# Making the convolution taps in 64 by 128 blocks instead of 32 by 64, with the tables laid out anew

## The chip, the cores and the metric

The kernel runs on one core of one Trainium2 chip, in one launch. The metric is the device time of an execution in microseconds (us), lower is better; three executions of the kernel before gave 542.96, 544.31 and 545.70 us, so the median is 544.31. A profile of one further execution shows what each engine did: PE is the matrix engine (PEld its weight loads), DVE the vector engine, ACT the scalar engine, POOL the general engine, SP the one that issues most DMAs.

## What is computed

The input is a sequence of 2048 positions and 448 channels. Two mixers work on it and a gate adds them:

```
q = (x @ wq).reshape(16 heads, 28);  k = x @ wk;  v = x @ wv      # one k and v for all heads
a = softmax(q k^T / sqrt(28)) v, heads side by side, @ wo
dt = exp(log_dt);  A = A_re + i A_im                              # 448 channels x 256 states
K[d, l] = Re sum_n C[d,n] * dt*B[d,n] * exp(dt*A[d,n] * l)        # 2048 taps for each channel
y[l, d] = sum_{m<=l} K[d, m] u[l-m, d]  +  Dskip[d] u[l, d]       # causal convolution
g = sigmoid(sum(x * gate_w));   out = g * a + (1 - g) * y
```

So there is an attention with 1024 score tiles (4 query blocks x 16 heads x 16 key tiles, each 128 keys by 512 queries), and a state space model whose 448 x 2048 taps are made first and then applied as a long convolution.

## The kernel before, in words

**Attention.** A loop over sets of three and two score tiles: PE multiplies keys by queries into PSUM (L1103 or L1112), ACT takes the exponential of the set in one instruction (L1134), PE multiplies by the values (L1144) into one bank. After 16 key tiles of four heads DVE copies the sums out (L1004), the denominators are inverted by way of POOL's DMAs (denT, R, rdenB), and DVE scales (L1014). `qproj` makes the queries of the next block, `outp` and `tail` multiply by `wo` (L986, L1055), and `fold` adds the gated result to O (L995).

**Convolution.** The 448 channels are worked in 14 chunks of 32. For each chunk:

- `masters` (L780, for a block of chunks) squares the complex numbers z = exp(dt A) again and again (L796 to L816), so that z to the powers 1, 2, 4 ... is at hand in bf16.
- `tables` (L820) builds on DVE, for 128 states in the partitions, two halves of states and 32 channels in the free dimension, the powers needed. Both the plain powers and those times C dt B stand in a table of rows, one row of EW = 128 elements for each of 32 exponents: 64 plain (half, channel) and 64 weighted. Real and imaginary part are two blocks, BLK = 33 rows apart. Five levels double the table: at each, L850 multiplies by the real part of a power, L852 by the imaginary part, and L854 and L856 subtract and add. The sizes go from 256 to 4096 elements (multiplications) and 128 to 2048 (additions). L859 and L863 build the decays `rho`, L867 multiplies them with the table in one instruction of 4096 elements (the mirrored powers, `Fm`), L872 changes a sign. Two tables alternate; `Fm` is there once.
- `kgen` (L875) makes the taps. The 2048 taps of a channel are the 32 by 64 outer product over 256 states, real and imaginary: four matmuls of 32 stationary columns (weighted powers) and 64 moving columns (plain and mirrored powers). Neighbouring columns are one row apart, 256 bytes. Four channels lie side by side in the four column groups of the array. A chunk takes 128 matmuls and fills one PSUM bank. DVE adds Dskip to one tap of each channel (L899) and copies the rest (L902) to `kstg`, and POOL issues nine DMAs that write them to DRAM (`KP_scratch`).
- `conv` (L937, twice a chunk) lets SP load the taps back as Toeplitz tiles, 1 MB for four channels (`tload`, into four buffers in T and, late in the run, three in U), and PE multiplies them with the input (L949) into a bank `ps`. DVE scales by 1 - g (L958) to `cst`, PE transposes by small matmuls (L969) into another bank `px`, DVE adds to O (L977).

**Order.** Nothing is ordered by hand. Each instruction is put on a list with its dependencies, an estimated duration and a priority `pr` (small is urgent: 0 for the scores, 1.4 taps, 1.6 convolution, 2 evictions, 50 and more for the tables), and `schedule` (L156) simulates the engines with these estimates and fixes the order of each engine before the program is emitted. `lock` and `unlock` hand out the two PSUM banks of POOL = (7, 5) (psX and the last of psS) that `qproj`, `kgen`, `conv`, `outp` and `prep` share; every other bank belongs to the attention. FETCH is its estimate for the loading of a block of 256 PE instructions while DMAs are running; SLACK is added to the time from which an instruction of priority 2 or more on an engine is taken to be ready. Real durations do not change the order: an engine stands where its next instruction must wait. At the end `tail` (L1040) writes O out.

Of the kernel before, what the change touches and what calls it, by code (L numbers as in the profile page):

```python
# [24 lines left out]
BLK = 33 * EW  # L25
LO = 2 * BLK
# [48 lines left out]
class Prog:  # L75
# [6 lines left out]
    BLOCK, FIRST, FETCH, IDLE, NEED = 256, 172, 5300.0, 3300.0, 0.015  # L82
# [3 lines left out]
    SLACK = {"pe": 500.0, "dve": 300.0}  # L86
# [289 lines left out]
class Kernel:  # L376
# [25 lines left out]
    def alloc(self):  # L402
        nc = self.nc
        sb = self.sb
        self.psS = self.ps("psS", 3072)
        self.psB = self.ps("psB", 512)
        self.psX = self.ps("psX", 512)
        self.psSb, self.psBb, self.psXb = self.psS.cast(BF), self.psB.cast(BF), self.psX.cast(BF)
        self.xT = sb("xT", XQ, BF)
        self.qM = sb("qM", 2 * 4 * 512, BF)  # L410
        self.kT = sb("kT", S, BF)
        self.vaug = sb("vaug", 512, BF)
        self.Wq = sb("Wq", NT * 512, BF)
        self.Wo = sb("Wo", NT * D, BF)
        self.Wb = sb("Wb", P, BF)
        self.ident = sb("ident", P, BF)
        self.qT = sb("qT", 2 * 512, BF)
        self.expT = sb("expT", RING * 512, BF)
        self.Wk = Sub(self.expT, (RING - 1) * 512)
        self.Wv = Sub(self.expT, (RING - 2) * 512)  # L420
        self.Wm = Sub(self.expT, (RING - 2) * 512 + 128)
        self.acc = sb("acc", 2 * 512, F32)
        self.rdenB = sb("rdenB", 512, F32)
        self.denT = sb("denT", 16, F32)
        self.onT = sb("onT", 4 * 512, BF)
        self.omq = sb("omq", 128, F32)
        self.U = sb("U", D * 32, BF)
        self.O = sb("O", 16 * D, BF)
        self.T = sb("T", NTR * TW + 768, BF)
        self.tab = sb("tab", 2 * LO + 32 * EW, BF)  # L430
        self.tmp = sb("tmp", 2 * 8 * EW, BF)
        self.rho = self.tmp
        self.mbf = sb("mbf", BM * MC, BF)
        self.mq = sb("mq", 5 * W2, BF)
        self.msq = sb("msq", 2 * 64 * BM, F32)
        self.msr = self.tmp.cast(F32)
        self.identf = self.msq
        self.seedz = sb("seedz", 2 * W2, F32)
        self.seedw = sb("seedw", 2 * W2, BF)
        self.kstg = sb("kstg", 2 * 256, BF)  # L440
        self.cst = sb("cst", 2 * 512, BF)
        self.skt = sb("skt", D // 4, BF)
        self.small = sb("small", 16, F32)
        self.gt = sb("gt", 2 * 16, F32)
        self.KP = nc.dram_tensor("KP_scratch", (2 * KH,), BF).ap()
        self.XS = nc.dram_tensor("XS_scratch", (3 * DT * XQ,), BF).ap()
        self.R = nc.dram_tensor("R_scratch", (16 * 4 * 512,), F32).ap()
# [37 lines left out]
    def loads(self):  # L485
# [57 lines left out]
        for k in range(2, 6):  # L543
# [4 lines left out]
        pg.dma([(self.skt.v(32 * g + 31, 1, 0, [[8, 14], [1, 8]]), dram(ins["B_Dskip"], 8 * g, [[16 * D, 1], [32, 14], [1, 8]]))  # L548
                for g in range(4)], (112, 8), "sk", rd=["skt"], wr=["skt"], pr=1, slow=True)
# [121 lines left out]
    def prep_params(self):  # L671
# [71 lines left out]
        for s in range(2):  # L743
            o = s * LO + 32 * EW
            for comp, val in ((0, 1.0), (1, 0.0)):
                pg.op("dve", lambda e, o=o, comp=comp, val=val: e.memset(self.tab.v(0, P, o + comp * BLK, [[1, 64]]), val), 70,
                      wr=[("lo", s, 0)] + xd, pr=3)
# [32 lines left out]
    def masters(self, b):  # L780
# [13 lines left out]
        for k in range(11):  # L794
# [20 lines left out]
            off = k * 256 if k < 5 else (k - 6) * 256 + 64  # L815
# [4 lines left out]
    def tables(self, c):  # L820
# [6 lines left out]
        mq = lambda lv: self.mq.v(0, P, lv * W2 + 64 * c, [[1, 64]])  # L827
        pr = 50 + 2 * c

        def vo(fn, n, rd, wr, rate=1.92):  # L830
# [3 lines left out]
        vo(lambda e: e.tensor_copy(tab.v(0, P, lo + 31 * EW, [[BLK, 2], [1, 64]]), mbf.v(0, P, mo, [[128, 2], [1, 64]])),  # L834
           128, [("mb", 0), lk(0)], [lk(1)])
        vo(lambda e: e.tensor_copy(tab.v(0, P, lo + 31 * EW + 64, [[BLK, 2], [1, 64]]),
                                   self.seedw.v(0, P, c * 64, [[W2, 2], [1, 64]])),
           128, [("w32", b), ("w32b", b), lk(0)], [lk(2)])
        done = [lk(1), lk(2)]
        for lv in range(5):  # L840
# [3 lines left out]
            so, do = lo + (32 - w) * EW, lo + (32 - 2 * w) * EW  # L844
            src = tab.v(0, P, so, [[BLK, 2], [EW, w], [1, EW]])
            dst = tab.v(0, P, do, [[BLK, 2], [EW, w], [1, EW]])
            mr = mbf.v(0, P, m, [[0, 2], [0, w], [1, EW]])
            mi = mbf.v(0, P, m + 128, [[0, 2], [0, w], [1, EW]])
# [3 lines left out]
            vo(lambda e, src=src, mi=mi, w=w, tb=tb, to=to: e.tensor_tensor(  # L852
                tb.v(0, P, to, [[w * EW, 2], [EW, w], [1, EW]]), src, mi, ALU.mult), 2 * n, done + mk(lv), [tk])
            vo(lambda e, do=do, n=n, tb=tb, to=to: e.tensor_tensor(  # L854
                tab.v(0, P, do, [[1, n]]), tab.v(0, P, do, [[1, n]]), tb.v(0, P, to + n, [[1, n]]), ALU.subtract), n, [tk, kr], [kr])
            vo(lambda e, do=do, n=n, tb=tb, to=to: e.tensor_tensor(  # L856
                tab.v(0, P, do + BLK, [[1, n]]), tab.v(0, P, do + BLK, [[1, n]]), tb.v(0, P, to, [[1, n]]), ALU.add), n, [tk, ki], [ki])
            done = done + [kr, ki]
        vo(lambda e: e.tensor_copy(rho.v(0, P, 31 * 64, [[1, 64]]), mq(0)), 64,  # L859
           [("mq", 0)], ["tmp"])  # L860
        for lv in range(5):
            w = 1 << lv
            vo(lambda e, w=w, lv=lv: e.tensor_tensor(rho.v(0, P, (32 - 2 * w) * 64, [[64, w], [1, 64]]),  # L863
                                                     rho.v(0, P, (32 - w) * 64, [[64, w], [1, 64]]),
                                                     self.mq.v(0, P, lv * W2 + 64 * c, [[0, w], [1, 64]]), ALU.mult), w * 64,
               [("mq", lv), "tmp"], ["tmp"])
        vo(lambda e: e.tensor_tensor(tab.v(0, P, FM, [[64, 2], [EW, 32], [1, 64]]),  # L867
                                     tab.v(0, P, lo + 31 * EW, [[BLK, 2], [-EW, 32], [1, 64]]),
                                     rho.v(0, P, 31 * 64, [[0, 2], [-64, 32], [1, 64]]), ALU.mult), 4096,
           done + ["tmp"], ["Fm"])  # L870
        ni = tab.v(0, P, lo + BLK + EW, [[EW, 31], [1, 64]])
# [3 lines left out]
    def kgen(self, c):  # L875
# [4 lines left out]
        G = self.grp()  # L880
        keys = self.tabkeys
        for jj in range(8):
            def mm(e, comp, jj=jj):
                for half in range(2):
                    for g in range(4):
                        o = half * 32 + 8 * g + jj
                        fo = lo + comp * BLK + EW + o
                        mo = FM + comp * 64 + o
                        r = e.matmul(  # L889
                            G.v(32 * g, 32, 64 * jj, [[1, 64]]),  # L890
                            tab.v(0, P, lo + comp * BLK + 64 + o, [[EW, 32]]),
                            tab.v(0, P, fo, [[mo - fo, 2], [EW, 32]]),
                            start=(comp == 0 and half == 0), stop=(comp == 1 and half == 1),
                            tile_position=(0, 32 * g), skip_group_check=True)
                return r
            for comp in range(2):
                pg.op("pe", lambda e, mm=mm, comp=comp: mm(e, comp), 226, mode="c", ni=16, rd=keys,
                      wr=[X, "kst", "kst2"], pr=1.4, lock=G if jj == 0 and comp == 0 else None)
        pg.op("dve", lambda e: e.tensor_tensor(self.kstg.v(0, P, 63, [[64, 8]]), G.v(0, P, 63, [[64, 8]]),  # L899
                                               self.skt.v(0, P, 8 * c, [[1, 8]]), ALU.add),  # L900
              el(8), rd=[X, "skt"], wr=["kst"], pr=2)
        pg.op("dve", lambda e: e.tensor_copy(self.kstg.v(0, P, 0, [[64, 8], [1, 63]]), G.v(0, P, 0, [[64, 8], [1, 63]])),  # L902
              el(504), rd=[X], wr=["kst2"], pr=2, unlock=G)
        ko = self.kstg
        rs = ko.rs
        lst = [(dram(self.KP, 32 * c * KW + 1024, [[8 * KW, 4], [KW, 8], [1, 64]]),
                bass.AP(tensor=ko.h, offset=16 * rs, ap=[[32 * rs, 4], [64, 8], [1, 64]]))]
        for g in range(4):
            for h in range(2):
                lst.append((dram(self.KP, h * KH + (32 * c + 8 * g) * KW, [[64, 16], [KW, 8], [1, 64]]),  # L910
                            ko.v(32 * g + 16 * h, 16, 0, [[64, 8], [1, 64]])))
        pg.dma(lst, (1056, 128), "kw", rd=["kst", "kst2"], wr=[("KP", c)], pr=0, eng="pool", extra=4000)
# [24 lines left out]
    def conv(self, c):  # L937
# [3 lines left out]
        ps, px = self.grp(), self.grp()  # L941
        for k in range(4):
# [3 lines left out]
            for n in range(8):  # L946
# [14 lines left out]
              el(512), rd=[X, "omq"], wr=[("cst", cs)], pr=2, unlock=ps)  # L961
# [12 lines left out]
        for k in range(4):  # L974
            pg.op("pe", lambda e, k=k: yt(e, k), 70, mode="h", ni=8, rd=[("cst", cs), "id"], wr=[Y], pr=1.55, lock=px if k == 0 else None)
# [4 lines left out]
    def outp(self, qc, tt):  # L980
# [4 lines left out]
        for g in range(4):  # L985
# [3 lines left out]
                rd=["Wo"] + [("on", gg) for gg in range(4)], wr=[X], pr=2, lock=G if g == 0 else None)  # L989
# [239 lines left out]
```

## Time and profile before

| | us |
|---|---|
| median of three executions | 544.31 |
| profiled execution | 546.33 |
| its span, first to last instruction | 544.5 |
| busy: ACT, DVE, PE | 485.9, 455.3, 451.6 |
| first exp to last exp (L1134) | 30.5 to 523.2 |
| DMA: 144.55 MB, mean rate | 265 GB/s |
| taps of the first chunk start, of the last end | 83.5, 484.8 |

A row of instruction groups reads: line, engine, operation, output <- inputs by the program's names, shapes (partitions x elements, type), count | busy us in all, mean ns of one | idle us of the engine just before them, and what ended it. For matmuls "128*32 128x64" is 128 rows by 32 stationary columns, and 128 by 64 moving. Of the chain that ended last, ACT has 30%, PE 27%, DVE 19% and DMA 15%.

### The profile page before, as it was taken

What the parts mean: (1) busy time and instruction counts of PE and PEld (TensorE: products, weight loads), DVE (VectorE), ACT (ScalarE), POOL (GpSimd) and SP (SyncE); (2) the same over time, 40 slices, a digit from 0 to 9 for tenths busy, and PEclk for the clock granted to TensorE, in tenths of its full rate; (3) what the DMA queues carried; (4) which work ended last, traced back from release to release, by engine and by line L of the source; (5) the groups of instructions that cost most, each with busy time, mean ns of one, the idle gap of its engine ahead of it and who ended that gap; (6) DMA issues with size and microseconds to landing.
All of it is one profiled execution on the core that took longest, in us unless ns stands there. A gap on an engine that the chain in (4) does not pass through costs nothing.

```text
span 544.5 us, 20905 instructions
## 1 busy us (share of the span) xinstructions
PE 451.6 (83%) x9463; PEld 226.4 (42%) x9479; DVE 455.3 (84%) x826; ACT 485.9 (89%) x431; POOL 168.1 (31%) x313
## 2 busy tenths in 40 slices
PE   4787679688798989789788898889898898996875
PEld 3522114154353535345344445345454444352443
DVE  2889999999999989889989998989899999912024
ACT  3699899999999989899999999999999998997840
POOL 5017022515142413315215241515225060532100
PEclk9958888999999999899999999999899999998888
DMA  8995691696977697896994998798994999679996
GB/s 254 238 232 151 47 159 30 172 355 206 360 238 247 189 368 244 257 365 216 361 373 136 362 308 305 208 390 273 326 371 144 345 337 353 182 258 321 361 385 194
DMA packets 122401, 144.55 MB, mean 265 GB/s; under 512 B 54196, under 2 KB 60956, under 8 KB 122312
## 3 DMA queue, kind: packets, MB, share of 16 engines
q1 hardware_dynamic: 112312, 133.06, 75.9%
q0 software_dynamic: 9344, 9.59, 7.3%
q8 instruction: 74, 1.21, 0.9%
q10 hardware_dynamic: 656, 0.57, 0.4%
q14 instruction: 15, 0.12, 0.1%
HBM read 128.76 MB, written 5.28 MB: 246 GB/s over the span
## 4 chain that ended last, share of the span: by engine, by line
ACT 30%; PE 27%; DVE 19%; DMA 15%; issue 3%; SPq 0%
ACT expT L1134 30%; DMA T<-KP_scratch 9%; PE psS L1112 6%; DMA U<-KP_scratch 6%; PE psX L889 5%; PE psS L1103 4%; PE psB L1144 4%; PE psS L949 2%; PE psX L949 2%; DVE msq L796 2%; DVE tab L850 2%; DVE mbf L816 2%; DVE seedz L800 1%; PE psS L889 1%; DVE tmp L852 1%
## 5 line engine op out<-in xcount | busy, mean ns | idle before, releaser
L1134 ACT ACTIVATE expT<-psS 128x1536 bf16<-128x1536 f32 (+1 forms) x410 | 468.1, 1317 | 23.1 <-PE psS L1112 11.7
L1112 PE MATMUL psS<-qM,kT 128*32 128x512 bf16 x1660 | 134.3, 400 | 14.0 <-ACT expT L1134 10.6
L1103 PE MATMUL psS<-qT,kT 29*128 29x512 bf16 x609 | 82.9, 400 | 33.4 <-ACT expT L1134 29.6
L1144 PE MATMUL psB<-expT,vaug 128*32 128x512 bf16 x1024 | 104.7, 398 | 0.7 <-issue 0.4
L135 POOL DMA_DIRECT2D KP_scratch<-kstg x126 | 67.8, 546 | 70.7 <-DVE kstg L902 69.2
L850 DVE TENSOR_TENSOR tab<-tab,mbf 128x256 bf16<-128x256 bf16 (+4 forms) x70 | 68.6, 979 | 0.7
L1103 PEld LDWEIGHTS psS<-qT,kT 29*128 29x128 bf16 x609 | 19.9, 91 | 83.3 <-ACT expT L1134 72.9
L135 POOL DMA_DIRECT2D rdenB<-R_scratch x60 | 30.6, 517 | 75.8 <-DMA R_scratch<-denT 56.3
L889 PE MATMUL psX<-tab 128*32 128x64 bf16 x1280 | 49.5, 286 | 0.3 <-issue 0.2
L1112 PEld LDWEIGHTS psS<-qM,kT 128*32 128x32 bf16 x1660 | 30.4, 98 | 45.6 <-ACT expT L1134 34.7
L1144 PEld LDWEIGHTS psB<-expT,vaug 128*32 128x32 bf16 x1024 | 27.4, 96 | 49.9 <-issue 38.2
L135 POOL DMA_DIRECT2D qM<-qT x64 | 32.1, 509 | 43.4 <-DVE gt L638 20.4
L889 PEld LDWEIGHTS psX<-tab 128*32 128x32 bf16 x1280 | 39.4, 135 | 11.3 <-issue 3.9
L949 PE MATMUL psX<-T,U 128*32 128x128 bf16 (+7 forms) x1568 | 34.4, 221 | 9.0 <-DMA T<-KP_scratch 5.9
L135 POOL DMA_DIRECT2D denT<-acc x15 | 11.3, 756 | 97.5 <-DVE acc L1004 97.5
L949 PE MATMUL psS<-T,U 128*32 128x128 bf16 (+7 forms) x1216 | 30.2, 222 | 9.5 <-DMA T<-KP_scratch 6.7
L852 DVE TENSOR_TENSOR tmp<-tab,mbf 128x256 bf16<-128x256 bf16 (+3 forms) x56 | 36.3, 648 | 0.0
L949 PEld LDWEIGHTS psX<-T,U 128*32 128x32 bf16 (+7 forms) x1568 | 26.5, 94 | 20.3 <-DMA T<-KP_scratch 8.1
L867 DVE TENSOR_TENSOR tab<-tab,tmp 128x4096 bf16<-128x4096 bf16 x14 | 32.1, 2290 | 0.4
L852 DVE TENSOR_TENSOR tab<-tab,mbf 128x4096 bf16<-128x4096 bf16 x14 | 31.9, 2278 | 0.0
L949 PEld LDWEIGHTS psS<-T,U 128*32 128x32 bf16 (+7 forms) x1216 | 21.7, 95 | 21.0 <-DMA T<-KP_scratch 6.9
L863 DVE TENSOR_TENSOR tmp<-tmp,mq 128x64 bf16<-128x64 bf16 (+4 forms) x70 | 25.3, 361 | 1.2
(153 smaller groups left out, 553.4 us busy)
## 6 DMA issues: line engine op xcount, KB each, us to landing
T<-KP_scratch SPq DMA_DIRECT2D x174, 512.0 KB, 9.3
U<-KP_scratch SPq DMA_DIRECT2D x50, 512.0 KB, 9.5
rdenB<-R_scratch POOLq DMA_DIRECT2D x60, 64.0 KB
U<-cst SPq DMA_DIRECT2D x1, 3584.0 KB, 19.0
qM<-qT POOLq DMA_DIRECT2D x64, 32.0 KB, 5.2
tab<-in_A_x_dram SPq DMA_DIRECT2D x4, 448.0 KB, 6.2
O<-in_A_x_dram SPq DMA_DIRECT2D x16, 112.0 KB, 2.7
O<-cst SPq DMA_DIRECT2D x1, 1792.0 KB, 27.1
```

Of the source, the lines that this page charges most:

```text
L135: return [e.dma_start(o, i, **kw) for o, i in pairs]
L796: pg.op("dve", lambda e: e.tensor_tensor(m2(msq), z2, z2, ALU.mult), el(2 * n), rd=[kr, ki] + first, wr=["msq"], pr=pr)
L850: vo(lambda e, dst=dst, src=src, mr=mr: e.tensor_tensor(dst, src, mr, ALU.mult), 2 * n, done + mk(lv), [kr, ki])
L852: vo(lambda e, src=src, mi=mi, w=w, tb=tb, to=to: e.tensor_tensor(tb.v(0, P, to, [[w * EW, 2], [EW, w], [1, EW]]), src, mi, ALU.mult), 2 * ...
L863: vo(lambda e, w=w, lv=lv: e.tensor_tensor(rho.v(0, P, (32 - 2 * w) * 64, [[64, w], [1, 64]]), rho.v(0, P, (32 - w) * 64, [[64, w], [1, 64]]),
L867: vo(lambda e: e.tensor_tensor(tab.v(0, P, FM, [[64, 2], [EW, 32], [1, 64]]), tab.v(0, P, lo + 31 * EW, [[BLK, 2], [-EW, 32], [1, 64]]), r ...
L889: r = e.matmul(G.v(32 * g, 32, 64 * jj, [[1, 64]]), tab.v(0, P, lo + comp * BLK + 64 + o, [[EW, 32]]), tab.v(0, P, fo, [[mo - fo, 2], [EW, ...
L949: r = e.matmul(ps.v(32 * j, 32 - 2 * n, 128 * k, [[1, 128]]), self.U.v(0, P, (4 * gi + j) * 32 + 2 * n, [[1, 32 - 2 * n]]), tbuf.v(0, P, t ...
L1103: r = e.matmul(self.psS.v(0, P, 512 * b, [[1, 512]]), kT.v(32 * h, DH + 1, 128 * kt, [[1, 128]]), qT.v(32 * h, DH + 1, 512 * (i % 2), [[1, ...
L1112: r = e.matmul(self.psS.v(32 * j, 32, 512 * b, [[1, 512]]), kT.v(0, P, 128 * kt + 32 * j, [[1, 32]]), self.qM.v(0, P, (i % 2) * XQ + 512 * ...
L1134: pg.op("act", lambda e: e.activation(expT.v(0, P, 512 * es[0], spread(es, n)), self.psS.v(0, P, 512 * bs[0], spread(bs, n)), AF.Exp, scal ...
L1144: r = e.matmul(self.psB.v(32 * h, 32, 0, [[1, 512]]), vaug.v(0, P, 32 * kt, [[1, 32]]), expT.v(0, P, 512 * ring[t], [[1, 512]]), start=(kt ...
```

## The change

The tables get another layout. A row now belongs to a pair of channels (and a half of the states) and holds all 32 exponents, each as two real and two imaginary parts: element 128 * row + 4 * exponent + 2 * part + channel of the pair. Rows 0 to 31 are weighted, rows 32 to 63 plain, so that the exponents of neighbouring pairs follow each other in steps of 4 elements (8 bytes) without a gap. Additions and the mirrored product now take two elements of every four; the mirrored product is split in two of 2048 elements, and a copy of 124 elements restores the entries for exponent 0 of the constant table.

A tap matmul takes 64 stationary columns (the 32 exponents of one channel in each of two pairs) and 128 moving columns (those two pairs, plain and mirrored), so its 64 by 128 result holds four blocks of 32 by 64, of which the two on the diagonal are taps of one channel. Two such matmuls lie side by side in two column groups. A chunk takes 64 matmuls and fills two banks, which are taken, evicted and given back one after the other; L899 and L902 come twice. The DMA that writes the taps becomes ten issues.

In `conv`, `px` is now the bank of `ps`. The projections in `outp` go from priority 2 to 1.2, FETCH from 5300 to 6200, SLACK of DVE from 300 to 500 ns. The core of the diff:

```diff
-    BLOCK, FIRST, FETCH, IDLE, NEED = 256, 172, 5300.0, 3300.0, 0.015
+    BLOCK, FIRST, FETCH, IDLE, NEED = 256, 172, 6200.0, 3300.0, 0.015
-    SLACK = {"pe": 500.0, "dve": 300.0}
+    SLACK = {"pe": 500.0, "dve": 500.0}
...
-            src = tab.v(0, P, so, [[BLK, 2], [EW, w], [1, EW]])
-            mr = mbf.v(0, P, m, [[0, 2], [0, w], [1, EW]])
+            src = tab.v(0, P, so, [[EW, 64], [2, 2 * w], [1, 2]])
+            dc = [tab.v(0, P, do + 2 * k, [[EW, 64], [4, w], [1, 2]]) for k in range(2)]
+            mr = mbf.v(0, P, m, [[2, 64], [0, 2 * w], [1, 2]])
...
+            tc = [tb.v(0, P, to + 2 * k, [[4 * w, 64], [4, w], [1, 2]]) for k in range(2)]
+            vo(lambda e, dc=dc, tc=tc: e.tensor_tensor(dc[0], dc[0], tc[1], ALU.subtract), n, [tk, kr], [kr])
+            vo(lambda e, dc=dc, tc=tc: e.tensor_tensor(dc[1], dc[1], tc[0], ALU.add), n, [tk, ki], [ki])
...
-        vo(lambda e: e.tensor_tensor(tab.v(0, P, FM, [[64, 2], [EW, 32], [1, 64]]),
+        for k in range(2):
+            vo(lambda e, k=k: e.tensor_tensor(tab.v(0, P, FM + 2 * k, [[EW, 32], [4, 32], [1, 2]]),
+                                              tab.v(0, P, lm + 124 + 2 * k, [[EW, 32], [-4, 32], [1, 2]]),
+                                              rho.v(0, P, 62, [[64, 32], [-2, 32], [1, 2]]), ALU.mult), 2048,
...
+        vo(lambda e: e.tensor_copy(tab.v(0, P, lm + EW, [[EW, 31], [1, 4]]), tab.v(0, P, lo + 64 * EW, [[0, 31], [1, 4]])),
+           124, done + ["Fm"], done)
...
+        for q in range(2):
+            G = self.grp()
+            for k in range(4):
+                m = 4 * q + k
...
+                                r = e.matmul(
+                                    G.v(64 * u, 64, 128 * k, [[1, 128]]),
+                                    tab.v(0, P, lo + cg * EW + 2 * comp + u, [[4, 64]]),
+                                    tab.v(0, P, fo, [[EW, 2], [mo - fo, 2], [4, 32]]),
...
+                pg.op("pe", mm, 230, mode="h", ni=16, rd=keys,
+                      wr=[(X, q), ("kst", q), ("ksk", q)], pr=1.4, lock=G if k == 0 else None)
...
-        ps, px = self.grp(), self.grp()
+        ps = px = self.grp()
...
-                rd=["Wo"] + [("on", gg) for gg in range(4)], wr=[X], pr=2, lock=G if g == 0 else None)
+                rd=["Wo"] + [("on", gg) for gg in range(4)], wr=[X], pr=1.2, lock=G if g == 0 else None)
```

## The prediction

> **What bounds the kernel now.** I read the busy times first, then the same by stage, the waits of the engines, the chain of waits, and the rows of the lines that the diff touches.
>
> ```profile
> PE 451.6 (83%) x9463; PEld 226.4 (42%) x9479; DVE 455.3 (84%) x826; ACT 485.9 (89%) x431; POOL 168.1 (31%) x313
> ```
>
> Three engines are within 6% of each other over the span. By stage (start:end, length, busy us and instructions of PE, PEld, DVE, ACT, POOL, then clock, DMA share, GB/s):
>
> ```profile
> 300.00:327.00 27.00, 25.26 (x539) 12.31 (x540) 26.24 (x45) 27.00 (x25) 9.57 (x17) 1.00 0.98 338
> 436.00:463.00 27.00, 23.60 (x569) 12.63 (x566) 24.54 (x39) 24.62 (x22) 9.47 (x19) 1.00 1.00 345
> 463.00:490.00 27.00, 25.85 (x615) 13.29 (x614) 14.97 (x23) 26.97 (x25) 11.43 (x22) 1.00 0.68 219
> 490.00:504.00 14.00, 8.83 (x160) 3.60 (x152) 3.85 (x7) 10.64 (x10) 3.98 (x8) 0.86 1.02 322
> ```
>
> Up to 477 us DVE and ACT are both nearly full and PE is close behind; after it DVE idles. There are two races. **Attention**: 410 exps run from 30.5 to 523.2 us with about 24.6 us of gaps between them; normalisation and output projection take the 21 us left. **The long convolution**: DVE makes the tables of 14 chunks one after another (the last step, L872, ends at 476.4), PE turns each into taps, POOL writes these to DRAM, SP loads them back as Toeplitz tiles, PE convolves. The last chunk's taps start at 477.2 and end at 484.8, and the chain after that is mostly loads, by the chain of waits (start, us, what):
>
> ```profile
> 491.68 11.99 DMA U<-KP_scratch
> ...
> 515.39 11.49 DMA U<-KP_scratch
> ...
> 538.74 0.61 PE psX L949 x32
> ```
>
> So what delays the tables delays the end, unless the 68 us behind them shrink. The DVE waits between 109 and 463 us (us in total, times, longest) show how little room DVE has:
>
> ```profile
> DVE cst L958 <- PE psS L949: 4.1, 3, 1.6
> DVE acc L1004 <- PE psB L1144: 3.5, 4, 1.7
> DVE O L977 <- PE psX L969: 2.3, 2, 1.6
> DVE O L995 <- PE psS L986: 1.8, 1, 1.8
> DVE cst L958 <- PE psX L949: 1.6, 4, 0.6
> DVE O L995 <- PE psX L986: 1.2, 1, 1.2
> ```
>
> With the smaller ones that is 16.3 us in 354; DVE stands only where the written order makes it await PE.
>
> **DVE, the added work.** The rows that price it (busy us, mean ns, idle before):
>
> ```profile
> L867 DVE TENSOR_TENSOR tab<-tab,tmp 128x4096 bf16<-128x4096 bf16 x14 | 32.1, 2290 | 0.4
> L854 DVE TENSOR_TENSOR tab<-tab 128x2048 bf16<-128x2048 bf16 x14 | 17.0, 1212 | 0.0
> L902 DVE CAST kstg<-psX 128x504 bf16<-128x504 f32 x10 | 6.7, 673 | 0.0
> L834 DVE COPY tab<-mbf 128x128 bf16<-128x128 bf16 x14 | 2.6, 186 | 0.0
> L899 DVE TENSOR_TENSOR kstg<-psX,skt 128x8 bf16<-128x8 f32 x10 | 1.9, 186 | 7.0 <-PE psX L889 6.9
> ```
>
> Two of the four blocks in each new product are unused, so a chunk fills two banks and is evicted twice: 673 + 186 = 859 ns more. The 4096-wide product becomes two of 2048: 2 x 1212 - 2290 = 134 ns. The new copy of 124 elements is one 186 ns copy. Together 1.18 us a chunk, x14 = 16.5 us, and 56 more instructions with the 7 ns that separate unheld ones (4.3 us in some 595 gaps) make 16.9. Nothing hides this: DVE is the engine that is full.
>
> **DVE, the same work in the new layout.** Element counts of the ten multiplications, ten additions, five decay steps and the sign change stay. Additions, the two products and the sign change now touch two adjacent bf16 and skip two (8-byte steps); multiplications read contiguous tables but a repeated pair as their factor. No row of before has such a DVE operand. Lower bound: nothing, as the type and the pairs stay. It is not less, since no operand of before has runs under 64 elements that could gain. Upper bound: one element a cycle instead of two, as in the f32 rows (682 - 414 ns for 256 elements, 1.05 ns each, against 0.52 in the bf16 rows, (1212 - 683)/1024). The skipping operations stream 2 x 3968 + 4096 elements a chunk, 6.2 us, so 6.2 us more a chunk, 87 us in all; the multiplications, 2 x 7936 elements, could add another 8.3 us a chunk. I take nothing: the nearest row is bf16 by two operands, L854. The few first levels may cost 50 ns each; they lie inside the range.
>
> [...]
>
> **PE.** Two timeline rows (start, us, line, times):
>
> ```profile
> 87.54 1.07 PE L889 MATMUL psS<-tab 128*32 128x64 bf16 x32
> ```
>
> ```profile
> 112.39 0.62 PE L949 MATMUL psS<-T,U 128*32 128x128 bf16 x32
> ```
>
> ```profile
> 131.02 0.45 PE L969 MATMUL psS<-ident,cst 128*64 128x64 bf16 x16
> ```
>
> Less the last one's 0.29, 0.22 and 0.20 us, a tap matmul costs 25 ns, a convolution one 13, a transposition one (two column groups, 64 stationary columns, as the new ones) 17. Today's taps, with elements 256 bytes apart, take 100 ns for four of 64 columns, 128 x 25 = 3.2 us a chunk. The new: 64 matmuls of 128 columns in two groups. At the convolution's rate a pair takes 52 ns, 26 each, 1.7 us; at today's strided rate 200 ns a pair, 6.4 us. I take twice the transposition's 17 ns, 34 ns: 2.2 us, a gain of 1.0 us a chunk, 14 us of PE time, because that row has the groups, the stationary width and a short step (4 bytes) in its moving operand. It is mostly off the path; where it is on it, it shortens ACT's and DVE's waits for PE. The pieces "issue" of 1.0 to 1.6 us on PE just behind the dense taps (336, 411, 455, 461 us) can shrink too: 128 of some 1,300 PE instructions a chunk go.
>
> **Other parts.** The tap write has ten issues instead of nine: 0.53 us more on POOL's queue a chunk, behind it the denT, qM and R transfers, before which POOL sits idle for longer than that (97.5 us in ten waits before denT alone); on the path only for the last chunk, 0.5 us. The convolution in one bank adds no wait: its transposition already awaits the eviction that frees the bank. But taps now need two banks in turn; where a convolution awaiting its load holds the other, the second half awaits an eviction queued behind up to 2.3 us of table work. Bounds of that: nothing, as with two free banks, and 14 x 2.3 = 32 us of later taps; I take nothing on the path, since DVE works on the next table meanwhile, and keep 2 us for the last chunk in the range. The planner's new constants move evictions 0.2 us later behind their producers: 21 DVE stalls x 0.2 = 4.2 us at least; with shorter PE bursts I take half of the 16.3 us, 8 us, bounds 0 and 16. The projection moved ahead of the convolutions frees its bank earlier and costs the same: nothing, bounds -2 and 2.
>
> **Sum**, against the profiled execution, 546.33 us (span 544.5): +16.9 (DVE) - 8 (stalls) + 0.5 (write) - 3.5 (last chunk's taps, 7.6 us long, in half the pieces between the attention matmuls, 1.0 of it PE time proper) = +5.9, 552.2 us. The median of the runs, 544.31, lies 2.0 below that execution: **550**.
>
> **Rivals.** (1) PE relief wins. Of ACT's gaps some 7 us are awaited "issue" or convolution bursts; if attention ends 7 us earlier, DVE loses no time to PE (all 16) and the 68 us after the tables shrink by 10, since the buffers that stand full from 479 to 488 us (DMA share 0.68) come free sooner: 16.9 - 16 - 10 = -9, **535**. For it: PE is 96% busy in 463:490 and the loads stall there. Against: convolutions still await the last tables. It decides once stalls and tail give back over 17 us. (2) The skipping DVE operands run at one element a cycle: 87 + 6 us less a tail of 20, about **615**; with part of it, 575 to 615. It decides from 0.4 us a chunk on. (3) The halved matmuls take no less time, as the change does not do what it says: at 50 ns each PE stays at 3.2 us, DVE's 16.9 come with no relief but the write's order: about 544.3 + 13 = **557**; at 100 ns PE gets 45 us more and the time goes to 575.
>
> **Chances.** The forecast 0.41 (543 to 555), rival 1 0.33 (531 to 542), rival 2 0.14, rival 3 0.12. A measurement here tells 0.5% from no change, that is 541.6 to 547.0. Below it lie rival 1 and little else, 0.34; within it the lower part of the forecast, 0.16; above it 0.50. The range runs from 531 to 580, which leaves out the far ends of rivals 1 and 2.
>
> **What would show it.** After: L902 and L899 twice as often at 0.67 and 0.19 us; the 2048-wide additions at 1.2 us (2.3 proves rival 2); tap matmuls about 34 ns apart (50 or more: rival 3); L872 of the last chunk near 485 us; DVE stalls near 8 us; from there to the end under 68 us. I am wrong if the tables end no later than 477 us, or if the time behind them shrinks by more than they are late.

## The result, and the profile after

The changed kernel takes **562.53 us** (median of four executions, 560.1 to 564.82) against 544.65 for the kernel before beside it: ratio 1.0331, 95% interval 1.0274 to 1.0388, so 3.3% slower. Its profiled execution took 560.1 us, with a span of 558.2, 13.7 more than before; all comparisons of profiles below are between these two spans, which lie some 4 us closer together than the medians. The mean granted clock was 0.935 (0.953 before); that does not explain 18 us, since the kernel before, run beside experiment 1, took 542.8 to 547.9 us at 0.928 to 0.952.

The busy line of the page (engine, busy us, share of the span, instructions):

```profile
PE 467.2 (84%) x8567; PEld 222.6 (40%) x8583; DVE 470.5 (84%) x882; ACT 489.4 (88%) x431; POOL 175.9 (32%) x327
```

PE has 896 instructions fewer and is busy 15.6 us **longer**; DVE has 56 instructions and 15.2 us more. The busy time by stage of the changed kernel, with the columns of the table shown for before:

```profile
300.00:327.00 27.00, 25.08 (x396) 9.61 (x397) 25.97 (x47) 26.84 (x25) 9.19 (x17) 1.00 0.74 240
436.00:463.00 27.00, 25.90 (x453) 11.91 (x454) 25.38 (x49) 25.49 (x24) 10.69 (x21) 1.00 0.86 283
463.00:490.00 27.00, 24.82 (x545) 12.79 (x533) 25.67 (x44) 25.95 (x24) 9.39 (x18) 1.00 0.88 300
490.00:504.00 14.00, 10.87 (x195) 4.06 (x195) 10.77 (x17) 12.68 (x12) 2.36 (x5) 0.83 0.93 313
```

In 300:327 and 436:463 PE is as busy as before or busier with a fifth to just over a quarter fewer instructions (396 for 539, 453 for 569). In 463:490 DVE is full (25.67 us), where before it had run out of tables (14.97): the tables now end in 490:504. L875, the sign change that ends a table (L872 before), ends for the last chunk at 502.8 us, 26.4 later than the 476.4 of before.

Which rows grew? Groups by shape (busy us, mean ns of one | idle before):

```profile
L868 DVE TENSOR_TENSOR tab<-tab,tmp 128x2048 bf16<-128x2048 bf16 x28 | 34.4, 1228 | 0.7
L898 PE MATMUL psX<-tab 128*64 128x128 bf16 x448 | 33.3, 303 | 0.2 <-DVE tab L875 0.2
L898 PE MATMUL psS<-tab 128*64 128x128 bf16 x448 | 33.5, 302 | 0.0
L856 DVE TENSOR_TENSOR tab<-tab 128x2048 bf16<-128x2048 bf16 x14 | 17.1, 1221 | 0.0
L912 DVE CAST kstg<-psX 128x504 bf16<-128x504 f32 x14 | 9.5, 676 | 0.0
L856 DVE TENSOR_TENSOR tab<-tab,tmp 128x128 bf16<-128x128 bf16 x14 | 3.9, 281 | 0.0
```

The DVE rows read as priced: the addition of 2048 in 8-byte steps takes 1221 ns (1212 before), an eviction 676. The surprise is L898: 33.5 + 33.3 = 66.8 us of PE for 896 tap matmuls, where the 1792 of before had 49.5 + 19.5 = 69.0. The mean of 303 ns is the duration of one matmul's record; as several are under way at a time, it says nothing of the pace. The pace is in a timeline row (start, us, engine, line, how many):

```profile
254.88 1.16 PE L898 MATMUL psS<-tab 128*64 128x128 bf16 x16
```

Less 0.30 for the last one, 15 follow each other in 0.86 us, 57 ns apart; over all such rows 57.7. A chunk has 64 of them: 3.7 us, against 128 x 23.4 = 3.0 us by all rows of before. Halving the matmuls made the taps 0.7 us a chunk longer.

DVE's waits between 109 and 463 us, the stretch shown for before (us in total, times, longest):

```profile
DVE kstg L908 <- PE psX L898: 8.6, 10, 1.6
DVE kstg L908 <- PE psS L898: 8.5, 9, 1.8
DVE O L986 <- PE psS L978: 2.4, 1, 2.4
```

The convolution's evictions (`cst`), which led the list before, have nearly gone from it. In their place DVE stands before L908, the first of each eviction pair, until the taps are done. From 109 us to the end of the last table its waits of over 0.15 us were 21, 17.1 us in all; now they are 34, 27.3 us. ACT waits more too, over the whole span. Before (L1112 multiplies `qM`, L1103 `qT`):

```profile
ACT expT L1134 <- PE psS L1112: 11.7, 13, 2.4
ACT expT L1134 <- PE psS L1103: 8.3, 12, 1.5
```

and after, where L1112 is the old L1103 and L1121 the old L1112:

```profile
ACT expT L1143 <- PE psS L1112: 22.2, 32, 2.5
...
ACT expT L1143 <- PE psS L1121: 6.5, 17, 1.3
```

Its gaps between exps grew from 24.6 to 32.5 us, and the last exp ends at 530.2 instead of 523.2. The chain of waits at the end (start, us, what):

```profile
512.39 17.28 ACT expT L1143 x15
...
540.21 8.15 DMA U<-KP_scratch
...
548.75 2.35 issue
551.11 1.69 PE psS L958 x53
```

ACT runs without a break from 512 to 530 us and only one load is left in this part of the chain. From the last table to the end it is now 55.4 us, 12.7 less than before. Most of that is a shorter queue of loads: the last 16 of the 224 Toeplitz loads, one chunk's, start 21.0 us after the last table instead of 29.7. So tables 26.4 us later, what follows 12.7 us shorter: 13.7 us of span.

### The profile page after: what moved, and what is told of

It reads as the page before. It is cut to its first block, busy times and chain, and to the rows that moved or that the text cites. A ratio compares the mean times of both kernels' runs of the same rounds, so it can differ in the third digit from the quotient of the medians.

```text
span 558.2 us, 19186 instructions
## 1 busy us (share of the span) xinstructions
PE 467.2 (84%) x8567; PEld 222.6 (40%) x8583; DVE 470.5 (84%) x882; ACT 489.4 (88%) x431; POOL 175.9 (32%) x327
## 4 chain that ended last, share of the span: by engine, by line
ACT 44%; PE 34%; DVE 10%; DMA 9%; issue 2%; SPq 0%; ACTq 0%
ACT expT L1143 44%; PE psS L1121 7%; DMA T<-KP_scratch 6%; PE psX L898 5%; PE psS L898 5%; PE psS L1112 4%; PE psB L1153 4%; PE psS L958 2%; DMA U<-KP_scratch 1%; DMA mbf<-in_A_wq_dram 1%; PE psX L958 1%; DVE msq L795 1%; PE psX L995 1%; DVE mbf L815 1%; PE psX L758 1%
## 5 line engine op out<-in xcount | busy, mean ns | idle before, releaser
L1121 PE MATMUL psS<-qM,kT 128*32 128x512 bf16 x1660 | 136.0, 405 | 17.6 <-ACT expT L1143 14.1
L1112 PE MATMUL psS<-qT,kT 29*128 29x512 bf16 x609 | 83.9, 405 | 41.4 <-ACT expT L1143 35.8
L134 POOL DMA_DIRECT2D KP_scratch<-kstg x140 | 76.4, 554 | 57.0 <-DVE kstg L912 39.7
L1112 PEld LDWEIGHTS psS<-qT,kT 29*128 29x128 bf16 x609 | 19.9, 91 | 96.4 <-ACT expT L1143 84.9
L1121 PEld LDWEIGHTS psS<-qM,kT 128*32 128x32 bf16 x1660 | 28.6, 97 | 59.7 <-ACT expT L1143 46.1
L958 PE MATMUL psS<-T,U 128*32 128x128 bf16 (+7 forms) x1600 | 37.5, 223 | 1.6 <-DMA T<-KP_scratch 0.9
L958 PE MATMUL psX<-T,U 128*32 128x128 bf16 (+7 forms) x1184 | 30.6, 231 | 5.9 <-DMA T<-KP_scratch 3.5
L868 DVE TENSOR_TENSOR tab<-tab,tmp 128x2048 bf16<-128x2048 bf16 x28 | 34.4, 1228 | 0.7
L958 PEld LDWEIGHTS psS<-T,U 128*32 128x32 bf16 (+7 forms) x1600 | 28.2, 95 | 14.7 <-issue 4.1
L898 PE MATMUL psX<-tab 128*64 128x128 bf16 x448 | 33.3, 303 | 0.2 <-DVE tab L875 0.2
L898 PE MATMUL psS<-tab 128*64 128x128 bf16 x448 | 33.5, 302 | 0.0
L898 PEld LDWEIGHTS psX<-tab 128*64 128x64 bf16 x448 | 24.7, 141 | 10.7 <-issue 7.1
L898 PEld LDWEIGHTS psS<-tab 128*64 128x64 bf16 x448 | 24.7, 141 | 10.0 <-issue 7.3
## 6 DMA issues: line engine op xcount, KB each, us to landing
U<-cst SPq DMA_DIRECT2D x1, 3584.0 KB, 19.5
```

The source lines that it names most:

```text
L134: return [e.dma_start(o, i, **kw) for o, i in pairs]
L868: vo(lambda e, k=k: e.tensor_tensor(tab.v(0, P, FM + 2 * k, [[EW, 32], [4, 32], [1, 2]]), tab.v(0, P, lm + 124 + 2 * k, [[EW, 32], [-4, 32 ...
L898: r = e.matmul(G.v(64 * u, 64, 128 * k, [[1, 128]]), tab.v(0, P, lo + cg * EW + 2 * comp + u, [[4, 64]]), tab.v(0, P, fo, [[EW, 2], [mo - ...
L958: r = e.matmul(ps.v(32 * j, 32 - 2 * n, 128 * k, [[1, 128]]), self.U.v(0, P, (4 * gi + j) * 32 + 2 * n, [[1, 32 - 2 * n]]), tbuf.v(0, P, t ...
L1112: r = e.matmul(self.psS.v(0, P, 512 * b, [[1, 512]]), kT.v(32 * h, DH + 1, 128 * kt, [[1, 128]]), qT.v(32 * h, DH + 1, 512 * (i % 2), [[1, ...
L1121: r = e.matmul(self.psS.v(32 * j, 32, 512 * b, [[1, 512]]), kT.v(0, P, 128 * kt + 32 * j, [[1, 32]]), self.qM.v(0, P, (i % 2) * XQ + 512 * ...
```

## The experiments

Three theories stood after the result. **Pace**: the tap matmuls follow each other at 58 ns instead of 34, and DVE and ACT wait for them. **DVE**: the 16.5 us of added DVE work is the loss, by itself. **Order**: the planner's estimates no longer fit, and engines stand at the wrong places. Where a kernel alters an estimate, an instruction count or a resource, the planner fixes the order anew; this is so in the first three runs and in those of the tables, the two banks and the split rows. The four runs that touch only addresses (contiguous operands, the eviction) keep the order of the changed kernel.

**1. The planner's estimate made true** (on the changed kernel). Eight tap matmuls are planned as 230 ns and take 8 x 57.7 = 462.

```diff
-                pg.op("pe", mm, 230, mode="h", ni=16, rd=keys,
+                pg.op("pe", mm, 460, mode="h", ni=16, rd=keys,
```

> The changed kernel with one number altered: the planner's estimate for a group of 8 tap matmuls goes from 230 to 460 ns, which is what the profile of the changed kernel shows (57.7 ns from start to start). Work and instructions stay. Theory 1 (DVE is full, its 16.5 us of added work is the loss): DVE's waits for the taps (L908, 26 us) may shrink, but the time stays above 555 us, since DVE still has 1.2 us more a chunk. Theory 2 (the order is wrong, because the taps take twice what the planner reckons): the waits for the taps fall from 26 to under 8 us, ACT's gaps from 31 to about 25 us, and the time falls by 10 us or more, to 552 us or less.

558.94 us beside 545.75, ratio 1.0265 (1.0221 to 1.0309); against the 562.53 of the changed kernel 3.6 us less. The waits did not go, they moved (over the whole span):

```profile
ACT expT L1143 <- PE psS L1121: 22.5, 14, 7.1
DVE kstg L908 <- PE psS L898: 19.9, 8, 5.4
```

Fewer waits, but long ones: 2.5 us each at L908, up to 7.1 us for ACT, and ACT's gaps grew to 36.3 us. DVE's waits up to the last table are 23.6 us, after 27.3. The true estimate gives back some 4 us, and the intervals of the two ratios overlap; the bulk of the loss is elsewhere.

**2. The three constants alone** (on the kernel before).

```diff
-    BLOCK, FIRST, FETCH, IDLE, NEED = 256, 172, 5300.0, 3300.0, 0.015
+    BLOCK, FIRST, FETCH, IDLE, NEED = 256, 172, 6200.0, 3300.0, 0.015
...
-    SLACK = {"pe": 500.0, "dve": 300.0}
+    SLACK = {"pe": 500.0, "dve": 500.0}
...
-                rd=["Wo"] + [("on", gg) for gg in range(4)], wr=[X], pr=2, lock=G if g == 0 else None)
+                rd=["Wo"] + [("on", gg) for gg in range(4)], wr=[X], pr=1.2, lock=G if g == 0 else None)
```

> The kernel before with only the planner's constants of the change: FETCH 6200, SLACK of DVE 500, projections at priority 1.2. If these constants carry part of the loss, it is slower than before by some of the 18 us; theories 1 and 2 both expect at most 0.5% either way, 542 to 547 us.

582.47 us, 1.0687 (1.0634 to 1.074): both expectations failed by far. Waits of this kernel:

```profile
DVE cst L958 <- PE psS L949: 22.9, 5, 8.6
DVE cst L958 <- PE psX L949: 14.3, 3, 11.4
```

In this order the convolutions come late (the last chunk's Toeplitz tiles load only at 544 to 561 us) and DVE stands up to 11.4 us before one eviction; nearly all of these waits lie behind the last table, which ends at 486.8. From there to the end it is 94.1 us, 26.0 more than before. So the constants are not a small tuning: with 128 tap matmuls a chunk they push the convolutions back. Runs 11 and 12 try them with other counts. Which of the three does it was not tried singly; that it is FETCH, which is charged for each block of PE instructions, is argued and not shown.

**3. DVE's added work alone** (on the kernel before): a second eviction pair, the product in two halves, a copy of 124 elements onto themselves.

```diff
-        vo(lambda e: e.tensor_tensor(tab.v(0, P, FM, [[64, 2], [EW, 32], [1, 64]]),
...
+        for k in range(2):
+            vo(lambda e, k=k: e.tensor_tensor(tab.v(0, P, FM + 64 * k, [[EW, 32], [1, 64]]),
...
+        vo(lambda e: e.tensor_copy(tab.v(0, P, lo + EW, [[1, 124]]), tab.v(0, P, lo + EW, [[1, 124]])), 124, done + ["Fm"], done)
...
+        pg.op("dve", lambda e: e.tensor_tensor(self.kstg.v(0, P, 63, [[64, 8]]), G.v(0, P, 63, [[64, 8]]),
+                                               self.skt.v(0, P, 8 * c, [[1, 8]]), ALU.add),
+              el(8), rd=[X, "skt"], wr=["kst"], pr=2)
+        pg.op("dve", lambda e: e.tensor_copy(self.kstg.v(0, P, 0, [[64, 8], [1, 63]]), G.v(0, P, 0, [[64, 8], [1, 63]])),
+              el(504), rd=[X], wr=["kst2"], pr=2)
```

> The kernel before with the change's added DVE work and nothing else of it: both evictions of the taps are done a second time, the mirrored product is split in two, and 124 elements are copied in place; 1.18 us a chunk, 16.5 us in all. Theory 1: slower by 12 to 17 us, 556 to 561 us, with the last tables at about 490 us. Theory 2: DVE's slack and the shorter end take most of it, slower by under 6 us, below 551 us.

558.39 us, 1.0248 (1.0198 to 1.0299): 12.6 us for 11.6 us more DVE busy time (466.9), last table at 494.6. Added DVE work costs about what it keeps DVE busy, as the theory of DVE said. That is some two thirds of the loss, and the taps run at before's pace here (24.9 ns). The busy time is less than the sum of the rows: the durations of all DVE records rose by 17.1 us, but a record mostly begins some 80 ns before the one ahead of it ends (in 615 of the 825 pairs of neighbours before), and with 56 more records that takes off about 5 us.

**4. Both tap operands contiguous** (on the changed kernel): the same counts and shapes, but 64 and 2 x 2 x 32 elements next to each other instead of in steps of 8 bytes.

```diff
-                                    tab.v(0, P, lo + cg * EW + 2 * comp + u, [[4, 64]]),
-                                    tab.v(0, P, fo, [[EW, 2], [mo - fo, 2], [4, 32]]),
+                                    tab.v(0, P, lo + cg * EW + 2 * comp + u, [[1, 64]]),
+                                    tab.v(0, P, fo, [[EW, 2], [mo - fo, 2], [1, 32]]),
```

> The changed kernel with the tap matmuls reading contiguous columns (step 1 instead of 4 elements), so they compute something else than the taps; order, counts and sizes stay. If the 8-byte step is what makes a tap matmul 57.7 ns, it falls to about 27 to 34 ns, which is also the planner's estimate. Theory 1: the time stays within 5 us of the changed kernel, 557 us or more. Theory 2: DVE's waits for the taps vanish and the time falls to 545 to 550 us.

545.01 us beside 545.75, ratio 0.9996 (0.9959 to 1.0032): **no loss is left**, with all of DVE's added work still there (468.5 us busy) and the order unchanged. The same timeline row:

```profile
250.93 0.68 PE L898 MATMUL psS<-tab 128*64 128x128 bf16 x16
```

(0.68 - 0.23) / 15 = 30 ns; over all 31.5. A chunk's taps take 2.0 us, 1.0 less than before and 1.7 less than in the changed kernel; DVE's waits to the last table fall from 27.3 to 14.1 us, ACT's gaps from 32.5 to 18.8, and the last table ends at 487.8, 15.0 earlier than in the changed kernel: 13.2 of these are the waits. From there to the end it is 56.0 us, as in the changed kernel. Over the whole span, the longest of the waits for the taps are now

```profile
DVE kstg L908 <- PE psS L898: 7.6, 3, 3.2
```

**5 and 6. One operand at a time** (on the changed kernel): the stationary side alone, then the moving side alone (the first, then the second changed line of the diff above).

> The changed kernel with only the stationary operand of the tap matmuls contiguous (it computes something else than the taps); order, counts and sizes stay. With both operands contiguous a tap matmul went from 57.7 to 31.5 ns and the time from 562.5 to 545.0 us. If the moving operand's step sets the pace (128 columns against 64), it stays near 55 ns and the time within 4 us of the changed kernel; if the weight load sets it, it falls to about 32 ns and the time to 545 to 550 us.

> The changed kernel with only the moving operand of the tap matmuls contiguous (it computes something else than the taps). If the moving operand's step sets the pace, a tap matmul takes about 32 ns and the time is 544 to 549 us; if the weight load does, 50 ns or more and 558 to 563 us.

Stationary alone: 559.85 us, 1.0257 (1.0212 to 1.0302). Moving alone: 543.0 us, 0.9981 (0.9941 to 1.0021). Their timeline rows, first with the stationary operand contiguous:

```profile
252.21 1.14 PE L898 MATMUL psS<-tab 128*64 128x128 bf16 x16
```

and then with the moving one:

```profile
248.72 0.71 PE L898 MATMUL psS<-tab 128*64 128x128 bf16 x16
```

The first is the pace of the changed kernel (56 ns; over all 55.4, although the weight loads shortened from 141 to 125 ns), the second that of contiguous operands (32 ns; over all 33.5). The **8-byte step of the moving operand** is what halves the pace.

Runs 3 and 4 fit together. From the changed kernel to run 4 the taps lose 14 x 1.68 = 23.5 us of PE time and the ratio falls from 1.0331 to 0.9996, 18.2 us: 0.77 us for each. With taps of before's length (3.0 us a chunk, 14 x 0.70 = 9.8 us less PE time than in the changed kernel) the change would thus lose 18.0 - 0.77 x 9.8 = 10.5 us, an estimate in a straight line; run 3 has 12.6. So, by this estimate, of the 18 us some 11 are DVE's longer work and some 7 are taps that became longer, where the prediction had 14 us of PE time gained.

**7. New tables, old blocks.** All of the new tables, but the taps as 128 matmuls of 32 by 64 in four column groups, one bank and one eviction, with the old constants and two banks for the convolution.

```diff
+        for jj in range(8):
...
+                        cg = half * 16 + ch // 2
+                        fo = lo + (32 + cg) * EW + 4 + 2 * comp + u
...
+                            G.v(32 * g, 32, 64 * jj, [[1, 64]]),
+                            tab.v(0, P, lo + cg * EW + 2 * comp + u, [[4, 32]]),
+                            tab.v(0, P, fo, [[mo - fo, 2], [4, 32]]),
...
+                            tile_position=(0, 32 * g), skip_group_check=True)
```

> The new tables with the matmul blocks of before: 128 tap matmuls of 32 stationary and 64 moving columns in four column groups, one bank, one eviction, nine DMA issues, the constants and the two convolution banks of before; the planner reckons 130 ns for eight tap matmuls instead of 226. DVE's added work is then 0.32 us a chunk instead of 1.18. If the step between columns sets the pace of a tap matmul, 8 bytes at about 0.9 ns a column make it 14 to 16 ns (25 before), PE saves 1.2 us a chunk, and the time falls to 530 to 543 us. If the number of matmuls or weight loads sets it, it stays near 25 ns and the time is 545 to 552 us.

550.76 us, 1.0085 (1.0048 to 1.0122). The pace came as in the first expectation, the time as in the second:

```profile
241.23 0.95 PE L894 MATMUL psS<-tab 128*32 128x64 bf16 x48
```

(0.95 - 0.24) / 47 = 15 ns, 62 ns for four of 64 columns, 2.0 us a chunk, and PE is busy 442.5 us, 9 less than before. But the time did not follow. DVE is busy 5.4 us more than before and waits 1.4 us more up to the last table, which ends 7.5 us later, at 483.9; what follows is 3.2 us shorter. Two rows (L954 is the convolution here, L963 its eviction) show PE's gaps and the late loads, one of the groups (idle before, and what ended it) and one of the waits:

```profile
L954 PE MATMUL psX<-T,U 128*32 128x128 bf16 (+7 forms) x1344 | 34.4, 222 | 11.1 <-issue 6.6 <-DMA T<-KP_scratch 4.5
```

```profile
DVE cst L963 <- PE psX L954: 25.8, 7, 10.9
```

"issue" is PE standing with nothing to wait for in the profile. Its pieces above 0.3 us add up to 21.7 us here, 10.9 before, 6.0 after and 0.8 in run 9. They go with PE's supply of instructions: in the trace's DMA packets, each of the 16 here ends 1.2 to 1.7 us after a 16 KB packet of the instruction queue q8 has landed, and so do 85 of the 88 in all runs. DVE's seven waits lie, but for 1.6 us, behind the last table, where it awaits convolutions that await loads. What the gaps cost in time was not measured.

**8. Two banks for the convolution** (on the changed kernel).

```diff
-        ps = px = self.grp()
+        ps, px = self.grp(), self.grp()
...
```

> The changed kernel with the convolution's transposition in a second bank, as before. Theory: the single bank is no part of the loss, since the transposition awaits the eviction anyway; the time stays within 1% of the changed kernel, 557 to 568 us. The rival, that holding one bank longer delays the taps' second half: faster by 5 us or more.

564.15 us, 1.0337 (1.0293 to 1.0381), as the changed kernel. The single bank has no part in the loss.

**9. Real and imaginary parts apart.** A row holds the two channels' real parts of all exponents and then the imaginary ones, so that a real or imaginary block is contiguous and holds 32 exponents of a channel pair. A tap matmul takes 64 of these on either side and the moving operand has no step.

```diff
-            src = tab.v(0, P, so, [[EW, 64], [2, 2 * w], [1, 2]])
+            src = tab.v(0, P, so, [[EW, 64], [64, 2], [1, 2 * w]])
...
-                            for u in range(2):
-                                cg = half * 16 + 2 * m
-                                fo = lo + (32 + cg) * EW + 4 + 2 * comp + u
-                                mo = FM + cg * EW + 2 * comp + u
+                            for v in range(2):
+                                cg = half * 16 + 2 * m + v
+                                fo = lo + (32 + cg) * EW + 2 + 64 * comp
+                                mo = FM + cg * EW + 64 * comp
...
-                                    tab.v(0, P, lo + cg * EW + 2 * comp + u, [[4, 64]]),
-                                    tab.v(0, P, fo, [[EW, 2], [mo - fo, 2], [4, 32]]),
+                                    tab.v(0, P, lo + cg * EW + 64 * comp, [[1, 64]]),
+                                    tab.v(0, P, fo, [[mo - fo, 2], [1, 64]]),
```

> The whole computation, with the changed kernel's matmul blocks and constants, but rows that hold real parts first and imaginary parts after them, each as 32 exponents of a pair of channels, so that both operands of a tap matmul and the additions read contiguous columns; a result block then holds the taps of one pair, sorted out by the eviction's read of every second PSUM column. One tiny copy more a chunk. Theory (the moving operand's 8-byte step is the loss): tap matmuls 31 to 34 ns, 541 to 548 us, level with before. If the contiguous variants were fast only for the numbers that they multiplied, it is above 555 us.

545.86 us beside 544.57, 1.003 (1.0001 to 1.006). Two rows, a small table step and the taps:

```profile
L851 DVE TENSOR_TENSOR tab<-tab,mbf 128x256 bf16<-128x256 bf16 x14 | 5.6, 399 | 0.0
...
L900 PE MATMUL psX<-tab 128*64 128x128 bf16 x608 | 26.5, 226 | 0.4 <-DVE tab L877 0.4
```

Pace 29.0 ns, "issue" pieces down to 0.8 us; on the other side the multiplication of 256 elements takes 399 ns instead of 289 in the changed kernel, and DVE has another small copy. Half as many tap matmuls without the step is level with the kernel before, and no better.

**10. One eviction cheaper** (on the changed kernel): the copy of the second bank reads a constant in SBUF and not the bank.

```diff
-            pg.op("dve", lambda e, o=o, G=G: e.tensor_copy(ko.v(0, P, o, [[64, 8], [1, 63]]), G.v(0, P, 0, [[64, 8], [1, 63]])),
+            pg.op("dve", lambda e, o=o, G=G, q=q: e.tensor_copy(ko.v(0, P, o, [[64, 8], [1, 63]]), self.ident.v(0, P, 0, [[0, 8], [1, 63]]) if q else G.v(0, P, 0, [[64, 8], [1, 63]])),
```

> The changed kernel with the copy of the second bank's taps (L912, half of them) made to read a constant in SBUF instead of PSUM, at the planner's old estimate, so the order is the same; half of the channels' taps are then wrong. DVE's part alone: 0.67 us become about 0.3, some 5 us over the run. If DVE's length sets the time of the changed kernel, it falls by 4 to 6 us, to 557 to 559 us; if the order waits on PE, by under 2 us.

559.93 us, 1.0273 (1.0238 to 1.0308), 2.6 us less than the changed kernel, between the two expectations and with overlapping intervals. It does not settle how much DVE's work costs in the changed order.

**11 and 12. The constants again, from both sides.** Run 7 with FETCH 6200, SLACK 500 and priority 1.2, and run 9 with 5300, 300 and 2.

> The run with the new tables and the old matmul blocks (550.8 us, 10 ns faster per tap matmul than before, yet PE waited 21.7 us for nothing that the profile shows), now with the planner's constants of the change: FETCH 6200, SLACK of DVE 500, projections at priority 1.2. Theory: its PE is starved of instructions, as it still has 128 tap matmuls a chunk; with a larger FETCH the planner knows of that, so PE's issue gaps fall below 8 us, but it then holds the convolutions back, as in the kernel before with these constants (582 us): 560 to 590 us. Rival: the constants suit the shorter taps, and the time falls below 545 us.

> The kernel with real and imaginary parts apart (contiguous tap operands, 64 tap matmuls a chunk, 545.9 us) with the planner's constants of before: FETCH 5300, SLACK of DVE 300, projections at priority 2. If the constants of the change fit the smaller number of PE instructions, it is slower, 550 to 565 us, with more issue gaps on PE than 1 us; if they matter little here, 543 to 549 us.

Run 11: 579.76 us, 1.0606 (1.0517 to 1.0695), where the same program with the old constants had 1.0085. In the profile, of the longest of its executions (583.01 us), the last chunk's loads come at 540 to 566 us, late as in run 2. With 128 quick tap matmuls as with 128 slow ones the new constants cost some 5%. Run 12: 548.24 us, 1.0034 (0.9993 to 1.0075), against 1.003 with the new ones: no difference in time, although "issue" pieces came back from 0.8 to 10.6 us and ACT's gaps grew to 25.2 us. With half the matmuls the program bears either set.

## Why the prediction was right, and where it was not

The direction and the mechanism of the sum (DVE's tables end later, the time behind them shrinks) held; its sizes did not. By the sum the last table ends 8.9 us later (16.9 - 8) and what follows is 3 us shorter; they became 26.4 and 12.7, and the second miss covers a good half of the first, which is luck. Term by term:

- **DVE, added work, +16.9 us.** The rows were right (L912 676 ns and L908 194 ns twice a chunk, products of 2048 at 1228), the sum of them too large: alone, in run 3, the added work keeps DVE busy 11.6 us longer, since neighbouring records overlap by some 80 ns. That busy time rose by 15.2 in the changed kernel is this and some 4 us of the next term, so the nearness to 16.9 is chance. The price in time was 12.6 us in run 3, and an estimate of 10.5 for all of DVE's longer work in the changed order; run 10, which took 4.6 us of busy time away and gained 2.6 within the noise, does not narrow it.
- **DVE, new layout, nothing.** Nearly right, and rival 2 was false: the additions in 8-byte steps took 1221 ns for 1212, the repeated pair as factor 2291 for 2288. The smallest steps rose, as the prediction allowed: the additions of 128 elements, with one word every 256 bytes, 281 ns for 220, the two copies of 128 elements to 234 and 247 for 186, the first steps of the decays 212 for 182 and 193 for 172; together some 4 us. Single words (two elements) 8 bytes apart thus ran at the rate of before in both sources and the destination (these 1221 ns). Longer times showed in the small steps just named and, in run 9, in the two multiplications of 256 elements, which read words 128 bytes apart there (399 ns for 289, 374 for 287).
- **The tap matmul, 34 ns, is the step that failed.** It was mis-sized: 57.7. The prediction took twice the rate of the transposition, whose moving operand steps 4 bytes, for one that steps 8 bytes, and had the range of 26 to 100 ns from the rows. A gain of 1.0 us a chunk was a loss of 0.7. The mechanism was the right one, that PE's time for the taps goes on to DVE and ACT: at 33.5 ns (run 6) the time is 543.0 us, below the 550 of the sum, and at 57.7 it is 562.5. (In run 6 the last table ends 9.2 us later than before, near the sum's 8.9, and what follows is 14.1 us shorter, not 3.) This is rival 3 ("the halved matmuls take no less time", at 50 ns 557, at 100 ns 575); interpolated between its two prices 57.7 gives 560, and it was 562.5. The cause is shown by runs 4 to 6: 57.7 ns as it is, 55.4 with the stationary side contiguous, 33.5 with the moving side, 31.5 with both.
- **Stalls, -8 us.** Wrong in sign, +10.2: they did not halve because their main source changed from the convolution's evictions to those of the taps. This hangs on the 34 ns, and not on the planner's estimate of 29: planned at 58 (run 1) the waits are still 23.6 us, run at 31.5 ns (run 4) they are 14.1, below before's 17.1 and still not half.
- **Behind the tables, -3 us (write and last taps).** The last taps themselves hardly changed, 7.4 us for 7.6; but the stretch lost 12.7 us. That is rival 1's item (10 us, as buffers come free sooner), and the sum had left it out: the loads that stood still in 463:490 before (DMA share 0.68) run in that stage now (0.88), 24 loads are issued behind the last table instead of 30, and the last chunk's start 8.7 us sooner after it. Why they do was not tried by itself; in runs 3, 4 and 6, whose tables also end 9 to 18 us later, the stretch is shorter too (60.4, 56.0 and 54.0 us).
- **Convolution in one bank, nothing.** Right (run 8, 1.0337 for 1.0331).
- **Constants, counted among the stalls at -4 to -8 us.** Not seen at all: they cost 37 us in the kernel before (run 2). With quick taps in rows split into real and imaginary parts they are worth nothing in time (runs 9 and 12).

So the forecast's own case (543 to 555) did not hold; the wider range did, through rival 3. With its pace the change would have been level with before (runs 4, 6 and 9, ratios 0.998 to 1.003): DVE's longer work, and what the quicker taps and the shorter end give back, cancel. Whether quick taps without DVE's work would gain stays open: run 7 comes nearest (DVE busy 460.7 us), and its order is its own, and so are its gaps on PE and late loads.

## What to carry to other kernels

Price a matmul by how its moving operand is read, not by its columns alone: before halving the number of matmuls by making each wider, find a row with the same step in bytes, or measure one, since here the step of 8 bytes (57.7 ns a matmul, 33.5 without it) stood between level and 3.3% slower. Where an order is planned from estimates, a slow operation does not become cheap by being planned truly: that gave back 3.6 of 18 us, with overlapping intervals. Try the constants of such a planner with each program by itself: here the same three cost 5 to 7% with 128 tap matmuls a chunk and nothing with 64. And to price a few more instructions on a full engine, look whether neighbouring records overlap, here by some 80 ns, before adding up their means.

## What the runs showed of the hardware that was not expected

- **PE's moving operand in steps.** In two column groups a matmul of 128 moving columns follows the next by 31.5 ns contiguous and 57.7 ns in 8-byte steps: 0.49 and 0.90 ns a column, as two run side by side. In four groups, 64 columns in 8-byte steps take 62 ns for four (0.98 a column), and before, with 256 bytes between the elements of both operands, 94 to 100 ns (about 1.5). The step of the stationary operand costs little: 57.7 to 55.4.
- **The same 8 bytes on DVE.** They cost it next to nothing (1221 ns for 1212), where PE's moving operand paid nearly twice for them (57.7 ns for 31.5).
- **PE's supply of instructions.** With 128 tap matmuls a chunk made quick (run 7) PE stood 21.7 us on "issue" in pieces over 0.3 us, with 64 of them (run 9) 0.8 us, with the constants that go with each count (10.6 with the others, run 12). 85 of the 88 such pieces in all runs end 1.2 to 1.7 us after a 16 KB packet of the instruction queue landed. One, of 2.35 us at 548.75, stands in the last chain of the changed kernel. The queue's packets fell from 74 to 67 with the change.
- **DVE's records overlap.** Of 825 pairs of neighbours before, 615 overlap, by some 80 ns: the durations add up to 505.2 us, the busy time to 455.3.
